# A dilated convolution with a gate: another order of the same instructions on five engines

## The chip, the cores and the metric

The kernel runs on one core of a Trainium2 chip. The metric is the device time of one execution in microseconds (us). A core has TensorE (PE in the profile, with its weight loads as PEld), VectorE (DVE), ScalarE (ACT), GpSimd (POOL) and SyncE (SP, which here only issues DMAs). Each engine works through its own instructions in the order in which they were written; engines wait for each other through semaphores.

## The reference

x is 2 x 16000 x 256, w is 3 x 256 x 512, w_o is 256 x 256, all bf16. A causal convolution of three taps, two time steps apart, is followed by a gate and a product:

```python
h = jnp.einsum('btc,cd->btd', xp[:, pad:pad + T, :], w[0])
for i in range(1, K):
    off = pad - i * dil
    h = h + jnp.einsum('btc,cd->btd', xp[:, off:off + T, :], w[i])
z = jnp.tanh(h[..., :D]) * _sigmoid(h[..., D:])
return z @ w_o
```

## The kernel before

Time is cut into 23 groups. A group of kind A has six phases of 256 time steps (18 groups), one of kind B four phases of 256 or 160 (4 groups); group 0 is done directly at the start. The convolution is computed by a short-convolution scheme that needs fewer products: sums and differences of the phases of x are multiplied by sums of the taps, and results are put together afterwards. A group has four blocks, one for each 128 of the 512 output channels.

A block of kind A goes through this, each letter being a token of the list below:

- F (PE) multiplies u1 by wa_sb into a PSUM bank "b"; c (ACT) copies it out as ss.
- M (PE) adds e (rm) times wm_sb into b; hh is then made from b, by h on DVE or by k on ACT.
- L (PE) adds f (rp) times wp_sb into b. A (DVE) makes a second bank "a" from ss and b. Y (DVE) makes yy from hh and b, or, after a k, from hh and a.
- Z (PE) adds u0 (r0) into b, once A and Y have read it; I (PE) adds u2 (ri) into a, once what reads a has read it.
- b, y and a (ACT) apply tanh or sigmoid to the three results.

A block of kind B has F, c, L, A, Z, I, b and a alone. Each of F, M, L, Z and I is two matmuls of up to 512 columns, here called a pair. After two such blocks g (DVE) multiplies th and sg into zz; P (PE) is four matmuls of 256 columns by w_o into a bank "o_ps"; e (ACT) or v (DVE) evicts it into osb; s (SP) stores, x (SP) loads by a transposing DMA. H and R are the last three P in two halves.

The operands of a group are tokens with a dot: `u2.7` is u2 of the A group with number 7. Written so, VectorE makes all of it. With `q` (`u2.7q22`) GpSimd makes one quarter, and not before the VectorE instruction that stands so many back has ended (`hold`). With `d` (`rm.15d`) GpSimd issues a DMA that adds one tile onto another: rm is e plus u3, rp is f plus u1, r0 is u0 plus uh, ri is u2 plus ud; u3, uh and ud are scaled copies of u1, made on VectorE. `wa.` are quarters of a weight sum. A GpSimd quarter after a DMA and a quarter waits for the one ahead of it (`settle`).

Three banks b, two banks a and three banks o_ps rotate; operands have three buffers (u3, uh, ud two), osb four.

What sets the order is one string, PLAN: 1730 tokens, read from left to right, each of which writes its instruction to its engine. Which block a letter stands for follows from ORDER, which gives the groups in turn. So the string sets the order on each engine, and also which of VectorE, GpSimd, GpSimd's DMA or ScalarE does a movable piece.

Of the kernel before, what the change touches and what calls it, by code (L numbers as in the profile page):

```python
# [22 lines left out]
wa.6q1 b L a G Z wa.14q10 F A b x wa.4q7 I c g P a d3.1 F L u1.0 c wa.0q1 Z A I b wa.13q1 P e.0 a Z f.0 F b P g I x
c uh.0 L e0 m.2 L d3.2q1 a F A e1 P d3.2q2 A c Z u0.0 I b I u3.0 a r0.0d Z u2.0 L p.2 b x d3.2q1 F e2 A P e3 F ud.0
c d0.2 Z a I u1.1 c L b g P d3.2q1 a L A e4 F wa.12q14 A Z wa.8q30 c e.1 I b Z g a L u1.2 b F wa.1q1 P e5 A ri.0d F
c rp.0 I e6 rm.0 L c s3 Z u3.1 a s2 M uh.1 s0 b uh.2 I x u2.1 k0 P a A F wa.7q1 e7 L u0.1 wa.9q11 P c A Z e8 wa.11q6
M ud.1 wa.15q28 b I Y k1 F f.1 a Z f.2 c I b L g x M a A F k2 u2.2 P u1.3q14 c L Y e9 M u1.3q54 A y I k3 rp.1d u3.2
P Y a Z L g e10 Z b A f.3q36 P y ud.2 F f.3q28 b Y P c r0.1d rm.1 P y Z ri.1d e.2 e11 F e.3 I b rm.2d M g c F k4 M
u0.2 u0.3q1 a L h5 c I y A f.3q12 L a M f.3q62 Y e12 P A u1.3q8 e13 Z I Y k6 u1.3q43 I b g ri.2d L a rp.2d F u3.3 y
Z A rm.3d c P u1.4 b r0.2d P a Y M rp.3d F y uh.3 Z ud.3 k7 v15 I b L u3.4 e14 ud.4 F f.4q68 c A P c M u0.3q20 Y a M  # L30
e.4 k8 Z k9 g L rm.4d b I u0.3q33 A e17 P a v16 F f.4q36 L y Y s8 P f.4q55 c x A Z y u2.4q74 M Y b I e18 h10 Z a F g
b P c L u2.3 F e19 u1.5 ri.3d M c A I u0.3q60 k11 M Y a L u0.4 y f.4q1 P A k12 I Z e20 r0.3d uh.4 Y P a rp.4d L b
f.5 r0.4d Z y A F b I g c P u2.5q72 y F Y M e21 u3.5 u2.5q4 I c v22 P y u2.4q90 h13 Z a u2.4q16 v23 M b L u2.4q50
h14 a s10 P s9 e24 u2.5q44 A F x y L Y e.5q82 P c A e.5q79 Z e25 Y M e.5q58 y I h15 b e.5q69 Z a g ri.4d F e26 L c I
A f.6q22 b P s11 uh.5 M a u2.5q82 Y F y rp.5d u0.5 P k16 Z e.6 e27 r0.5d L b g I c P u2.6q118 A y F M e28 u1.6q63 Y
P c f.6q1 h17 Z y I ud.5 e29 rm.5 M b s12 L h18 a u2.6q1 x F a P u2.6q45 A c L Y u1.6q20 e30 I A u1.6q108 e31 M Z a
Y u1.6q33 P k19 g ri.5d Z b L e32 u0.6 P f.7q89 y A I b F uh.6 u2.6q46 e33 P Y c F r0.6d u3.6 P y g rm.6d M e34 I
f.6q13 a h20 P c Z y u1.7 L f.6q67 b M A e35 P rp.6d Y F k21 s14 P a e.7 s13 Z c ud.6 I g e36 ri.6d L b M u2.7q71 A
e37 P a h22 F u0.7q137 e38 P Y u0.7q65 c L s15 Z y uh.7 x u2.7q72 A M b I f.7q90 h23 e39 F f.7q1 y Y L c f.7q114 I
v40 a Z u2.7q22 Y a M g P b P k24 A F e41 x L rp.7 e42 P c A Z y u1.8 I u0.8q93 b M Y a P u0.7q161 h25 Z y F uh.8 b  # L40
u3.7 I u2.8 s16 c rm.7d F e43 f.8 M c L g rp.8d k26 M a u2.7q76 A L k27 Y I y u0.8q1 A Z a u0.7q103 P v44 b u0.8q81
L Y y s17 P u0.8q162 A e45 F r0.7d e46 Z ud.7 Y c I ri.7d P b u3.8 r0.8d M u1.9 a Z e.8 k28 F b ud.8 L rm.8d e.9 c I
y g F u2.9q179 M y A P c P e47 h29 f.9q46 M a Y s18 f.9q43 L e48 s1 ri.8 u2.9q60 Z x k30 I A b L u2.9q117 Y a F y
u0.9q14 A Z c I g u0.9q1 b P a M Y F y u0.9q167 h31 I e49 ud.9 Z c u3.9 L b e.10 rm.9d M e50 A P u0.9q89 a F s19 h32
e51 I x Y f.9q75 c P g L a f.9q1 Z e52 Y P b M u0.10q72 A e53 F u1.10 Z c I h33 y P uh.9 b M f.10 s20 r0.9d y L h34
u2.9q136 F e54 A P a L c Y u0.10q111 I y Y u0.10q129 M e55 Z A rp.9d k35 P uh.10 ri.9d b Z g a I L e56 ud.10 u3.10 F
b s21 A P a x F u2.10 c P Y c M y u1.11 Z e57 M h36 b I u3.11 e58 L g u2.11q137 k37 F P a A L y Y u2.11q107 P c A
u2.11q42 Z y I f.11 rm.10d y M Y b u0.10q118 P e59 v60 rp.10d Z k38 s22 F uh.11 r0.10d b g P a L u0.11 c F P e61 A I
e62 ud.11 ri.10q1 M c Y P y r0.11d u1.12 Z y rp.11d M h39 b I e.11 e63 L u3.12 a F ri.10q1 h40 P e64 A P c ri.10q52
L e65 Y u2.11q33 M a s24 g ri.10q10 Z k41 x I b A L a F u2.12q103 Y y I u2.12q220 A c Z uh.12 rm.11d P y Y P b g M y  # L50
s23 F k42 v66 I u1.13q121 c Z v67 a ri.11d L f.12 e68 M b P A s25 e.13q152 P k43 x Y F a e.13q125 L c e.12 u1.13q170
Z e69 A I b M f.13 u1.13q1 e70 P Y a F u2.12q52 P v71 k44 Z c rp.12d g L y rm.12d M b A I k45 ud.12 P u2.13q69 Y a
s26 F e72 u0.12 L u2.13q15 c Z A P y u2.13q63 M Y b I u1.13q210 e73 h46 F a u2.12q15 Z c uh.13 rp.13d I g y L ri.12d
b M ud.13 P A k47 e.14q113 F a Y L c e.13q247 I A y Z e.14q191 e74 M Y e.13q189 P b h48 Z r0.12d y u3.13 F a g L
rm.13d b I f.14 c P u2.14q103 y F A e75 M v76 u0.13q202 I c h49 P u0.13q57 e77 M Y a u2.14q55 s28 L e78 h50 x
u0.13q102 Z a Y P u2.13q15 b L A e.14q70 y P y F u1.14 u0.13q101 Z A c I b ri.13d Y M e79 s27 F r0.13d u3.14 k51 g Z
c I u1.15 a L M b A f.15q131 P a u3.15 F f.15q226 e80 Y P k52 s29 e.15 P c x L g e81 Z y M A u0.15q78 b I h53
e.14q248 P y F Y e82 u2.15q170 L a u0.14 u2.15q128 Z c P Y b I u2.15q278 A e83 M rm.14d a ud.14 F h54 e84 Z rp.14d
uh.14 I c g L r0.14d b P e85 u2.14q287 A M y P Y e86 P h55 u2.14q38 y F u1.16 a Z ri.14d I g b L c P Y f.16q41 e87 F
e88 A M f.16q231 c P h56 u0.15q120 e89 Z v90 M a f.15q216 s32 L b s30 h57 u0.15q75 I x y A f.16q213 F a L Y f.15q45  # L60
y P uh.15 u0.15q94 c Z A e91 I s31 u2.15q110 Y M b P rm.15d g a F k58 rp.15d Z u3.16 c uh.16 L y u2.16 M b I ud.15 A
k59 P ri.15d F a ud.16 r0.15d Y L y P d0.3q55 c A Z e92 M Y b I u1.17 e93 d0.3q1 Z a h60 I m.3q93 b F e.16 ri.16d L
c g F rm.16d y P e.17q121 A c M e94 P h61 e95 M e.17q79 Y I a s34 f.16q22 L h62 s33 a Z A e96 d3.3q1 P y d0.3q64 Y P
e.17q45 b L g Z y rp.16d F b d3.3q40 Y I c P d3.3q65 A e97 F m.3q78 u0.16 e98 d0.3q252 M c I s35 h63 r0.16d Z a
u3.17 M e99 f.17 P b h64 L rp.17d a P A y u0.17q176 F e100 Y L y P d3.3q161 A u0.17q101 c Z Y I e.17q58 b I e101 g M
rm.17d a F s36 u2.17q5 h65 y P s4 s7 Z c g p.3q78 s5 L b M A e102 P u0.17q112 k66 Y F u2.17q17 a P v104 c L m.3q26
uh.17 p.3q67 Z e103 A M p.3q36 b s37 ud.17 I m.3q10 k67 Y P u0.17q286 a F v106 p.3q135 y L r0.17d Z c A P u2.17q16 y
M Y b I u2.17q30 e105 h68 Z a v107 F ri.17q5 b L ri.17q4 s38 y I A ri.17q3 P c Y F y ri.17q28 M c g Z a P h69 b P g
e108 M L e109 h70 F y I A c P a Y L I y Y Z a A M b P h71 y Z v110 F b L c I A F a L Y P c A I e113 v111 Z a L v112
Z b P A b s40 I g y s39 P a F I v114 c F P g c L a Z e115 A L P v116 b I e117 A Z s41 P g a s6 I b v118 Z a P b P  # L70
e119 g H P v120 s42 R P e121 H e123 v122 H R s44 R e124 s43 e125 s45
"""


# [572 lines left out]
```

## Time and profile before

| | |
|---|---|
| median of 3 runs | 258.78 us (258.61 to 259.19) |
| profiled execution | 258.77 us, span 256.6 us |
| granted TensorE clock | 0.995 |
| DVE busy | 242.8 us, 405 instructions |
| ACT busy | 243.7 us, 492 instructions |
| POOL busy | 176.9 us, 249 instructions |

The span runs from the first to the last instruction; the profiled execution has 2.2 us around it. A row of the timeline gives start and length in us, engine, line, operation, the written tile and the read ones, the shape, and the number of instructions that were merged; in brackets stands the engine's idle time ahead of it and what ended it. A row of the groups by line gives busy time and mean length in ns, then idle time ahead of the group and what ended it.

### The profile page before, as it was taken

How to read it: one execution, taken by the hardware profiler on the slowest of the kernel's cores; microseconds unless marked ns; L12 is line 12 of the kernel's file. 1: busy time of each engine (PE TensorE's matmuls, PEld its weight loads, DVE VectorE, ACT ScalarE, POOL GpSimd, SP SyncE). 2: the span in 40 equal slices, each digit the busy share in tenths (PEclk: the TensorE clock that was granted, in tenths of full speed). 3: DMA queues.
4: the chain of work that ended last, by engine and by line, in shares of the span. 5: the costliest groups of instructions: out<-in, count | busy, mean ns of one | idle time of the engine just before them, and what ended most of it. 6: DMA issues, size and time to landing. Idle time of an engine off the chain costs nothing.

```text
span 256.6 us, 4575 instructions
## 1 busy us (share of the span) xinstructions
PE 249.9 (97%) x1428; PEld 138.0 (54%) x1428; DVE 242.8 (95%) x405; ACT 243.7 (95%) x492; POOL 176.9 (69%) x249
## 2 busy tenths in 40 slices
...
GB/s 184 213 202 213 196 172 159 232 143 203 187 199 271 187 200 249 182 289 200 200 237 212 249 196 188 290 244 147 212 260 171 216 219 224 198 217 102 0 226 176
DMA packets 84320, 51.73 MB, mean 202 GB/s; under 512 B 69032, under 2 KB 70312, under 8 KB 84296
## 3 DMA queue, kind: packets, MB, share of 16 engines
...
q10 hardware_dynamic: 912, 0.95, 1.1%
q8 instruction: 11, 0.18, 0.3%
q14 instruction: 13, 0.11, 0.1%
...
## 4 chain that ended last, share of the span: by engine, by line
PE 82%; DVE 8%; DMA 3%; ACT 2%; issue 2%; ACTq 0%; DVEq 0%
PE b L359 48%; PE o_ps L478 18%; PE a L359 13%; DVE a L393 2%; DMA e<-u 2%; DVE zz L460 2%; DVE yy L393 2%; PE b L379 1%; PE a L379 1%; DMA xn<-in_x_dram 1%; DVE hh L393 1%; ACT osb L495 1%; ACT sg L441 1%; ACT th L441 0%; ACT ss L390 0%
## 5 line engine op out<-in xcount | busy, mean ns | idle before, releaser
L330 POOL TENSOR_TENSOR u<-xt 128x256 bf16<-128x256 bf16 x88 | 66.8, 774 | 15.0 <-PE b L359 8.4
L478 PE MATMUL o_ps<-wo_sb,zz 128*128 128x256 bf16 x496 | 72.0, 273 | 0.0
L495 ACT CAST osb<-o_ps 128x512 bf16<-128x512 f32 x101 | 63.8, 646 | 0.9 <-PE o_ps L478 0.7
L478 PEld LDWEIGHTS <-zz 128*128 128x128 bf16 x496 | 48.5, 98 | 27.6
L393 DVE SCALAR_TENSOR_TENSOR a<-ss,b 128x512 f32<-128x512 f32 (+1 forms) x88 | 59.5, 679 | 2.3 <-PE b L359 1.3
L390 ACT COPY ss<-b 128x512 f32<-128x512 f32 (+1 forms) x88 | 55.0, 628 | 0.9 <-PE b L359 0.6
L359 PEld LDWEIGHTS <-w_sb 128*128 128x128 bf16 x352 | 34.1, 97 | 35.1 <-issue 3.0
L359 PE MATMUL b<-e,wm_sb 128*128 128x512 bf16 x144 | 42.8, 379 | 0.3 <-DMA e<-u 0.3
L359 PE MATMUL b<-u,w_sb 128*128 128x512 bf16 x144 | 42.9, 379 | 0.2
L359 PE MATMUL b<-u,wa_sb 128*128 128x512 bf16 x144 | 42.9, 379 | 0.0
L359 PE MATMUL b<-f,wp_sb 128*128 128x512 bf16 x144 | 42.9, 379 | 0.0
L359 PE MATMUL a<-u,w_sb 128*128 128x512 bf16 x144 | 42.5, 379 | 0.3 <-DVE a L393 0.2
L460 DVE TENSOR_TENSOR zz<-th,sg 128x1536 bf16<-128x1536 bf16 (+2 forms) x46 | 41.3, 897 | 0.2
L441 ACT ACTIVATE th<-b 128x512 bf16<-128x512 f32 (+1 forms) x44 | 28.0, 636 | 1.4 <-ACT ss L390 0.7
L441 ACT ACTIVATE th<-a 128x512 bf16<-128x512 f32 (+1 forms) x44 | 28.6, 649 | 0.3 <-PE a L359 0.2
L441 ACT ACTIVATE sg<-b 128x512 bf16<-128x512 f32 (+1 forms) x44 | 28.0, 635 | 0.6 <-PE b L359 0.5
L441 ACT ACTIVATE sg<-a 128x512 bf16<-128x512 f32 (+1 forms) x44 | 28.3, 642 | 0.0
L359 PEld LDWEIGHTS <-wm_sb 128*128 128x128 bf16 x176 | 17.0, 98 | 17.2 <-DMA e<-u 1.2
L359 PEld LDWEIGHTS <-wp_sb 128*128 128x128 bf16 x176 | 16.9, 98 | 17.3 <-issue 1.6
L393 DVE SCALAR_TENSOR_TENSOR hh<-ss,b 128x512 f32<-128x512 f32 x38 | 25.9, 681 | 0.2
L393 DVE SCALAR_TENSOR_TENSOR yy<-hh,b 128x512 f32<-128x512 f32 x38 | 25.6, 678 | 0.0
L441 ACT ACTIVATE sg<-yy 128x512 bf16<-128x512 f32 x36 | 24.9, 693 | 0.7 <-DVE yy L393 0.7
...
## 6 DMA issues: line engine op xcount, KB each, us to landing
...
u<-uh POOLq DMA_DIRECT2D x18, 256.0 KB, 4.8
f<-u POOLq DMA_DIRECT2D x16, 256.0 KB, 4.7
u<-ud POOLq DMA_DIRECT2D x15, 256.0 KB, 4.6
e<-u POOLq DMA_DIRECT2D x15, 256.0 KB, 4.8
out_dram<-osb SPq DMA_DIRECT2D x8, 256.0 KB, 3.1
w_sb<-in_w_dram ACTq DMA_DIRECT2D x3, 256.0 KB, 4.1
xt<-in_x_dram SPq DMA_TRANSPOSE x22, 8.0
```

The lines of the kernel that those rows point to most:

```text
L330: ins = eng.tensor_tensor(out=o, in0=a, in1=b, op=op)
L359: nc.tensor.matmul(G[bank, oi][:, :2 * R], lhsT=wmat[:, ct, osl], rhs=G[mv][:, :, ct, :R], start=which == "first" and ct == 0, stop=ct == ...
L379: nc.tensor.matmul(G[bank, oi][:, :4 * r].rearrange("p (j r) -> p j r", j=4), lhsT=w_taps[tap][:, ct, osl], rhs=xt[:, j0:j0 + 4, ct, c0 + ...
L390: nc.scalar.copy(out=G["ss", oi][:, :n], in_=G["b", oi][:, :n])
L393: return note(nc.vector.scalar_tensor_tensor(out=out, in0=in0, scalar=scalar, in1=in1, op0=ALU.mult, op1=op))
L441: nc.scalar.activation(out=G[name, dt][:, j:j + 2, :R], in_=G[bank, oi][:, :2 * R].rearrange("p (q r) -> p q r", q=2), func=(ACT.Tanh, ACT ...
L460: note(nc.vector.tensor_tensor(out=G["z"][:, dt, :, :n], in0=G["th", dt][:, :, :n], in1=G["sg", dt][:, :, :n], op=ALU.mult))
L478: nc.tensor.matmul(o_ps[:, q, :], lhsT=z, rhs=wo_sb[:, dt, :], start=dt == 0 and (q == 0 or len(dts) == NT), stop=dt == NT - 1, skip_group ...
L495: copy(out=G["osb", at][:, 2 * jp:2 * jp + 2, :], in_=o_ps[:])
```

## The change

PLAN is replaced by another string of 1730 tokens. Groups, ORDER, buffers and functions stay. The diff's first line of the string:

```
-m.0 d3.0 p.0 F F d0.0 c F c G L w L A c D wa.5q2 D A wa.2q5 Z d0.1 I b D m.1 a L wa.3q1 F d A wa.10q2 Z c p.1 I
+m.0 p.0 d0.0 F F c G D c D d3.0 L w L A D wa.7q4 F A wa.2q6 d Z G I b p.1 Z c F m.1 a I d0.1 c L d3.1 b P wa.6q1 L a
```

By count of tokens, all of F, M, L, Z, I, P, H, R, c, A, Y, b, y, a, g, s and x are as many as before. These differ:

| token | before | after |
|---|---|---|
| h / k (hh on VectorE / ScalarE) | 38 / 34 | 36 / 36 |
| e / v (eviction on ScalarE / VectorE) | 103 / 23 | 102 / 24 |
| d3 whole / quarters | 2 / 8 | 3 / 4 |
| u0 whole / quarters | 10 / 32 | 11 / 28 |
| u2 whole / quarters | 7 / 44 | 5 / 52 |
| r0 by DMA / VectorE | 18 / 0 | 17 / 1 |
| rm by DMA / VectorE / quarters | 15 / 3 / 0 | 14 / 3 / 4 |
| ri by DMA / VectorE / quarters | 15 / 1 / 8 | 17 / 0 / 4 |

VectorE between hh and A of the second block of the A group with number 7, before (numbers are those of buffers):

```order
L393 SCALAR_TENSOR_TENSOR hh_1595<-ss_1569,b_1553 128x512
L328 TENSOR_SCALAR uh_1603<-u1_1576 128x1024
L328 TENSOR_SCALAR u3_1607<-u1_1406 128x1024
L330 TENSOR_TENSOR u2_1611<-xt_1284 128x1024
L330 TENSOR_TENSOR f_1621<-xt_1284 128x1024
L460 TENSOR_TENSOR zz_1536<-th6_1532,sg6_1582 128x1536
L393 SCALAR_TENSOR_TENSOR a_1637<-ss_1569,b_1553 128x512
L393 SCALAR_TENSOR_TENSOR yy_1643<-hh_1595,b_1553 128x512
```

And after:

```order
L393 SCALAR_TENSOR_TENSOR hh_1587<-ss_1564,b_1552 128x512
L328 TENSOR_SCALAR ud_1596<-u1_1379 128x1024
L487 CAST osb6_1602<-o_ps_1581 128x512
L393 SCALAR_TENSOR_TENSOR yy_1615<-hh_1587,b_1552 128x512
L393 SCALAR_TENSOR_TENSOR a_1623<-ss_1564,b_1552 128x512
L328 TENSOR_SCALAR uh_1632<-u1_1542 128x1024
```

Five instructions stood between hh and A; now three do, and Y is one of them.

GpSimd ahead of the DMA that makes rm of the A group with number 15 (`e<-u`), before:

```order
L330 TENSOR_TENSOR f<-xt 128x256 x2
L330 TENSOR_TENSOR u_2712<-xt 128x256
L330 TENSOR_TENSOR f<-xt 128x256
L330 TENSOR_TENSOR u_2712<-xt 128x256
L330 TENSOR_TENSOR f<-xt 128x256 x2
L330 TENSOR_TENSOR u_2712<-xt 128x256
L330 TENSOR_TENSOR u_2733<-xt 128x256
L325 DMA e<-u_2671 128x1024
```

And after:

```order
L330 TENSOR_TENSOR f<-xt 128x256
L330 TENSOR_TENSOR u_2749<-xt 128x256
L330 TENSOR_TENSOR u_2715<-xt 128x256 x2
L330 TENSOR_TENSOR u_2749<-xt 128x256
L330 TENSOR_TENSOR f<-xt 128x256 x3
L325 DMA e<-u_2828 128x1024
```

Nine quarters stood between it and the DMA before it; now eight do, and in the list the DMA stands 1.3 us of PE work further ahead of its M.

ScalarE at the very end, before:

```order
L495 CAST osb_3564<-o_ps 128x512
L495 CAST osb_3612<-o_ps 128x512
L493 CAST odd<-o_ps 128x256
L495 CAST osb_3636<-o_ps 128x512 x2
L642 UNCONDITIONAL_BRANCH
```

And after:

```order
L495 CAST osb_3609<-o_ps 128x512 x2
L493 CAST odd<-o_ps 128x256
L495 CAST osb_3636<-o_ps 128x512
L642 UNCONDITIONAL_BRANCH
```

The second half of the last tile (osb_3636) has left ScalarE; it is VectorE's last instruction after.

More of the change, by code (lines that the diff above doesn't have):

```diff
@@ L21 @@
 PLAN = """
-m.0 d3.0 p.0 F F d0.0 c F c G L w L A c D wa.5q2 D A wa.2q5 Z d0.1 I b D m.1 a L wa.3q1 F d A wa.10q2 Z c p.1 I
[L23 to L71, printed above, removed]
+m.0 p.0 d0.0 F F c G D c D d3.0 L w L A D wa.7q4 F A wa.2q6 d Z G I b p.1 Z c F m.1 a I d0.1 c L d3.1 b P wa.6q1 L a
@@ new lines @@
+A F wa.0q7 A x wa.4q6 I c g Z a L u1.0 b Z A e0 I b P u2.0 F a f.0 F c ud.0 Z c g L b I u0.0 wa.3q1 L A a F wa.8q22
+e1 A P wa.12q5 P c s0 m.2 Z e2 x e3 I d0.2 L b u3.0 Z a p.2 wa.1q1 F b A P c I g e4 Z d3.2 F b u1.1 I x a L e.0 c F
+A a P wa.9q1 c ud.1 L uh.0 I e5 u3.1 wa.5q1 Z A a L wa.14q37 b uh.1 P wa.10q3 A Z e6 ri.0d F g x b Z f.1 c I rm.0 b
+F L rp.0 c I u1.2 a M a P g k0 F A wa.13q1 e7 P e.1 L c wa.11q45 Z e8 A s2 I rp.1d b s3 r0.0 M a F Y wa.15q1 k1 P
+u2.1 c Z e9 g L ri.1d M b A y F uh.2 k2 P Y u1.3q19 c I u0.1 e10 L Z a u2.2 x u1.3q1 P y A M b u0.2 I k3 F Y a L
@@ new lines @@
+rm.1 c Z f.3q25 y I A M b r0.1d u3.2 P Y a F k4 e.2 Z c g L rm.2d b M e11 u1.3q40 A I e12 F h5 y P u1.3q1 Y L a P
+ud.2 c f.2 Z e13 M g b x u0.3q1 I k6 F A a L f.3q10 Y c I f.3q51 A e14 P y M uh.3 rp.2d Y Z a ri.2d P k7 u3.3 Z
+r0.2d u1.4 b L e.3 b F f.4q69 y A F c I v15 c f.3q31 P Y a M f.4q65 v17 M e16 rp.3d I k8 g Z rm.3d k9 L ud.3 a P
+u3.4 u2.4q1 b A L y F Y u0.3q12 y P A u0.3q36 c Z e18 I u0.3q80 Y M y e.4 r0.3d Z b P h10 a rm.4d F u2.3 b L c u1.5
+F x e19 M g c I e.5q62 k11 A M a L Y u2.4q35 y I A e.5q51 k12 P Z y Y f.4q9 L a uh.4 ri.3d I b f.5 Z s8 e20 u2.5q101
@@ new lines @@
+A F b P s9 u0.4 f.4q53 c P Y e21 F r0.4d g y M Z c rp.4d h13 P a u2.5q68 M v22 b L e23 F ud.4 y u2.4q16 h14 P c I
+u2.5q1 A e24 L u2.4q82 Y a M Y I u2.5q30 e25 Z k15 A e.5q80 P a uh.5 ri.4d Z b ud.5 L g y F f.6q13 e26 I A c P s11
+u3.5 u1.6q85 y P s10 Y M b ri.5d u0.5 Z a rp.5d F g k16 I b L e.6 u2.6q45 c P A e27 F e28 M u1.6q70 Y c P u1.6q117
+h17 y Z f.6q98 v29 M e30 L b f.6q8 h18 s12 I a x u1.6q61 Y F y L u2.6q35 A a P e.5q11 Y c Z e31 A P f.6q110 M b rm.5
+r0.5d I y g rp.6d F k19 Z a e.7 L c I u0.6 f.7q84 b P A e32 P uh.6 e33 M f.7q112 Y F a r0.6d u1.7 P e34 Z c h20 I
@@ new lines @@
+e35 g L b u2.7q72 s14 M a Y x F y P A u2.6q29 y P h21 Z c u3.6 P e36 g rm.6d L b I u0.7q28 e37 A F e38 P uh.7 c
+u2.6q26 Y s15 M e39 s13 M f.7q1 h22 a Z f.7q40 y I ud.6 L b u2.7q140 h23 P y u0.7q40 A F a L u2.7q50 Y e40 I c A
+u0.7q53 Z a M Y rp.7d b P u1.8 ri.6d k24 Z u3.7 y F g rm.7q77 L y I c A P e41 M rm.7q36 Y b s16 P u0.7q52 h25 a x Z
+y ud.7 F rm.7q1 v43 L b P u0.8q41 e42 Y F c u2.7q6 A I c M ri.7d uh.8 a e.8 Z r0.7d k26 M x g b I k27 L f.8 u0.8q1 F
+y A P a L u3.8 e44 Y P rm.7q1 c P A e45 f.9q10 Z e46 Y M u0.8q92 b I u2.8 rm.8d k28 Z u1.9 rp.8d F a I g b L y
@@ new lines @@
+u2.9q57 F A c P e47 f.9q72 M Y c P s18 u0.8q6 h29 e48 Z a uh.9 M ud.8 L b e.9 ri.8d I k30 A F f.9q78 y L Y a r0.8d I
+g c Z y M A b P h31 e49 P e50 F Y u0.9q1 L a s19 u1.10 Z c u2.9q39 s17 P A e51 M b u2.9q16 Y I y f.9q48 h32 F e52 P
+e.10 rp.9d c Z u3.9 a I g rm.9d M b L e53 u0.9q64 h33 F y s20 P u3.10 c u0.9q139 x Y P a M u0.9q69 A y L u2.9q145
+h34 e54 Z I Y y u2.10q25 L b uh.10 u2.10q8 P A a F u0.10q114 y Y Z c r0.9d A I b M g e55 Z k35 I e.11 a F ud.9 L b
+f.10 ri.9d P c A F u0.10q42 a M Y c P u0.10q115 e56 h36 Z y M u1.11 s21 b x L g k37 I F e57 A u2.11q167 P a u3.11
@@ new lines @@
+u0.10q68 L c Y I e59 u2.11q105 A M a Z u2.11q8 v58 k38 P Y u2.10q50 y P b L f.11 rp.10d Z y g rm.10d F e60 rm.11d I
+b A P u2.10q70 c v61 F a r0.10d M Y e62 P h39 y Z s23 u1.12 c I s6 L s22 b ud.10 x P ud.11 y ri.10q121 A F e63 M Y
+ri.10q45 c P a u0.11 ri.10q47 Z e64 M h40 b I uh.11 k41 L g u2.12q115 F a L A c P u2.12q172 Y y P e65 ri.10q57 A M y
+Z v66 u2.11q176 I k42 Y u2.12q83 P b L g rp.11d a Z y ri.11d F f.12 b P ud.12 u1.13q163 c I A e67 F Y a u1.13q222 M
+P c e.12 r0.11d Z k43 u0.12 M b rp.12 L e.13q1 k44 F A e68 I c v69 e.13q135 L s25 a P s24 Y u1.13q27 M e70 u3.12
@@ new lines @@
+u1.13q185 Z y A P k45 rm.12d g I b L e71 u2.13q159 Y F a P s26 f.13 e.13q157 c x Z A e72 I e.13q240 b M Y P a
+u2.13q66 h46 F y uh.12 Z c ud.13 L r0.12d uh.13 b M g rp.13d y I k47 e.14q27 F A P e73 Y L a u2.12q104 I v74 e75 Z c
+e.14q177 A s27 P y e.14q11 M Y b P u2.13q39 h48 a Z ri.12d f.14 e76 F b P u3.13 g L c rm.13d F y e.14q241 Y M c I
+h49 e77 M u0.13q123 y A P s28 u0.13q149 a x L h50 u0.13q237 y Z A L e78 u2.13q151 Y I b u2.14q121 P Y a F u0.13q81 y
+A Z c r0.13d I g b Z ri.13d M a u1.14 F b e.15 P rp.14d k51 F u3.14 c u1.15 L rm.14d e79 M A c u2.14q8 I e80 P Y k52
```

14 lines of the change are left out of this document (added).

## The prediction

> **What bounds the kernel now.** First the page, for the engines' shares and the chain.
>
> ```profile
> span 256.6 us, 4575 instructions
> PE 249.9 (97%) x1428; PEld 138.0 (54%) x1428; DVE 242.8 (95%) x405; ACT 243.7 (95%) x492; POOL 176.9 (69%) x249
> PE 82%; DVE 8%; DMA 3%; ACT 2%; issue 2%; ACTq 0%; DVEq 0%
> ```
>
> Three engines are nearly full, and the chain stays on PE for 82% of the span. A busy PE is not yet a full one, because matmuls overlap, so next I read starts in the timeline of PE (start, length, what), and counts in the groups by line.
>
> ```profile
> 5.22 2.63 PE L379 MATMUL b<-xt,w_sb 128*128 128x320 bf16 x18
> 7.68 0.45 PE L242 MATMUL tp<-ident,xn 80*128 80x80 bf16 x8
> 43.28 0.60 PE L478 MATMUL o_ps<-wo_sb,zz 128*128 128x256 bf16 x4
> 43.72 0.60 PE L359 MATMUL b<-u,w_sb 128*128 128x512 bf16 x2
> 44.15 0.60 PE L359 MATMUL b<-f,wp_sb 128*128 128x512 bf16 x2
> 250.20 1.47 PE L478 MATMUL o_ps<-wo_sb,zz 128*128 128x256 bf16 x12
> ...
> L478 PE MATMUL o_ps<-wo_sb,zz 128*128 128x256 bf16 x496 | 72.0, 273 | 0.0
> L478 PEld LDWEIGHTS <-zz 128*128 128x128 bf16 x496 | 48.5, 98 | 27.6
> L359 PE MATMUL b<-u,wa_sb 128*128 128x512 bf16 x144 | 42.9, 379 | 0.0
> L359 PE MATMUL b<-m,wm_sb 128*128 128x512 bf16 x24 | 6.8, 379 | 0.0
> L379 PE MATMUL a<-xt,w_sb 128*128 128x320 bf16 x24 | 3.8, 300 | 0.0
> ```
>
> From 43.72 to 44.15 a pair of 512 columns takes 0.432 us, from 43.28 to 43.72 four of 256 take 0.436, and from 5.22 to 7.68 eighteen of 320 take 0.137 each. Five groups of 144 and four of 24 make 408 pairs: 176.3 us. The 500 of 256 columns (496 and 4) make 54.5, the 80 of 320 columns 11.0, eight transposes 0.3. That is 242.1 us of work. It stands between 5.22 and 251.51 (250.20 and twelve times 0.109), which is 246.3. So PE stands still for some 4.2 us; this, and the 5.1 us from 251.51 to the end, is all that another order can shorten, since no matmul is added or taken away. The work before 5.22 has the same places in both lists.
>
> A rule weighed against this: the Trainium skill (Perfetto Trace Analysis, Identifying the Most-Contended Engine) says that matmul busy share is a bad measure and that the busy share of LDWEIGHTS and the share of peak FLOPs are good ones. By the first of these, 54% here, PE would have nearly half its time free; by its peak of 307.2 G elements a second, 571,392 columns by 128 in 256.6 us are an estimated 93%. The starts above side with the second, and the sum would otherwise have no floor.
>
> Where do the 4.2 us lie? A start later than the pitch allows is a gap. Those above 0.035 us, taken along the whole timeline:
>
> ```profile
> 42.31 0.59 PE L359 MATMUL b<-e,wm_sb 128*128 128x512 bf16 x2
> 42.85 0.59 PE L359 MATMUL a<-u,w_sb 128*128 128x512 bf16 x2
> 110.86 0.59 PE L359 MATMUL b<-f,wp_sb 128*128 128x512 bf16 x2
> 111.63 0.59 PE L359 MATMUL a<-u,w_sb 128*128 128x512 bf16 x2 [0.18 <-DVE a L393]
> 237.66 0.59 PE L359 MATMUL a<-u,w_sb 128*128 128x512 bf16 x2
> 238.25 0.59 PE L359 MATMUL b<-u,w_sb 128*128 128x512 bf16 x2
> ...
> 107.54 0.68 DVE L393 SCALAR_TENSOR_TENSOR hh<-ss,b 128x512 f32<-128x512 f32 x1
> 109.42 0.69 DVE L330 TENSOR_TENSOR f<-xt 128x1024 bf16<-128x1024 bf16 x1
> 110.02 0.95 DVE L460 TENSOR_TENSOR zz<-th,sg 128x1536 bf16<-128x1536 bf16 x1
> 110.89 0.69 DVE L393 SCALAR_TENSOR_TENSOR a<-ss,b 128x512 f32<-128x512 f32 x1
> ```
>
> First kind: Z and I, which wait for VectorE's A and Y. There are 13 such gaps, 2.03 us together, the first at 42.85 (0.11), the largest at 111.63 (0.34), the last at 238.25 (0.16). At 111.63 VectorE had finished hh at 108.2 and then did u-sums, f and zz before A.
>
> ```profile
> 12.59 1.07 PE L359 MATMUL b<-p,wp_sb 128*128 128x512 bf16 x4
> 13.50 0.71 PE L379 MATMUL a<-xt,w_sb 128*128 128x320 bf16 x4
> 202.79 0.59 PE L359 MATMUL b<-f,wp_sb 128*128 128x512 bf16 x2
> 203.28 0.59 PE L359 MATMUL b<-e,wm_sb 128*128 128x512 bf16 x2
> ```
>
> Second kind: F, M and L, which wait for ScalarE's copies and activations or for hh. 17 gaps, 1.41 us, from 13.50 (0.05) to 203.28 (0.06).
>
> ```profile
> 48.91 0.59 PE L359 MATMUL b<-e,wm_sb 128*128 128x512 bf16 x2
> 49.45 0.61 PE L359 MATMUL b<-f,wp_sb 128*128 128x512 bf16 x2
> 205.88 0.59 PE L359 MATMUL b<-u,w_sb 128*128 128x512 bf16 x2
> 206.81 0.61 PE L359 MATMUL b<-e,wm_sb 128*128 128x512 bf16 x2 [0.34 <-DMA e<-u]
> 201.43 0.87 POOL L325 DMA_DIRECT2D e<-u  x1
> e<-u POOLq DMA_DIRECT2D x15, 256.0 KB, 4.8
> ```
>
> Third kind: three waits for an accumulating DMA, 0.69 us: 0.11 at 49.45, 0.07 at 161.49, 0.50 at 206.81, where the issue at 201.43 was 5.4 us ahead.
>
> **The change part by part.** Only the list moves. By its tokens VectorE gets as many sums, two hh fewer and one eviction more: 0.6 us less at its steps (0.60 from f at 109.42 to zz, 0.87 from zz to A). ScalarE gets two hh more and one eviction fewer, 0.5 us more. I cost both at nothing, because each still has less to do than PE; should VectorE fall behind, its 0.6 us is already in the next term. GpSimd has 160 quarters of operands and 64 DMAs, as before.
>
> To compare the lists I count, for each edge, the PE work that stands between the producer's place and its consumer's. A tight edge has one pair or less, 0.432 us, while a VectorE operation takes 0.68.
>
> Z and I after A or Y: 20 tight edges before (14 for Z, 6 for I), 12 after (9 and 3). 2.03 us over 20 is 0.10 each; eight fewer give -0.81. Its ends are 0, if VectorE's total load and not the order makes the gaps, and -2.03. I take the count, because at 111.63 the delay was visibly work put ahead of A, and after has there only one ud, an eviction and Y.
>
> F, M and L after ScalarE or hh: 75 tight before (22, 30, 23), 91 after (37, 34, 20). 1.41 over 75 is 0.019 each; sixteen more give +0.30. Ends: 0 and +1.3, if every new one costs what the mean gap does (0.083).
>
> DMAs: the three late ones get longer leads (6.06, 6.06, 4.33 us become 9.52, 14.29, 5.63), which takes 0.69 away. New short leads stand at r0.1 and r0.16 (both 4.33 us). Before had three at 4.33 and one of them cost 0.50, so 0.17 each: +0.34. Net -0.35; ends -0.69 and +0.31 (two times 0.50).
>
> Last quarters: rm.7 and ri.10 now end on GpSimd 0.87 us of PE work ahead of M and I; before, the nearest such were 1.30 and 1.73, and cost nothing.
>
> ```profile
> L330 POOL TENSOR_TENSOR f<-xt 128x256 bf16<-128x256 bf16 x28 | 20.8, 754 | 3.5 <-PE b L359 2.8
> 127.82 2.02 POOL L330 TENSOR_TENSOR f<-xt 128x256 bf16<-128x256 bf16 x2
> 198.80 1.30 POOL L330 TENSOR_TENSOR f<-xt 128x256 bf16<-128x256 bf16 x2
> 128.22 1.08 DVE L460 TENSOR_TENSOR zz<-th,sg 128x1536 bf16<-128x1536 bf16 x1
> ```
>
> A quarter takes 0.75 and fits into 0.87 if GpSimd starts it at its place. I take +0.15, a little over the nearer end, 0; the other is the first rival's. rm.7's last quarter also waits for u3 on VectorE, and f.9's quarter stands behind it with long leads.
>
> The end:
>
> ```profile
> 249.88 0.69 DVE L487 CAST osb<-o_ps 128x512 bf16<-128x512 f32 x1
> 251.49 1.07 ACT L495 CAST osb<-o_ps 128x512 bf16<-128x512 f32 x2 [0.34 <-PE o_ps L478]
> ```
>
> Two evictions run one behind the other on ScalarE until 252.56, then the last store. After puts the last on VectorE. PE's last matmul ends at 251.67 (twelve steps and the drain, 250.20 and 1.47), so it would run from about 251.71 for 0.69, until 252.40: -0.15. Ends: -0.5, a whole one of ScalarE's two, and +0.2, what VectorE's 0.69 is above that. Stores and loads on SP keep their number and sizes and I cost their moves at nothing, covered by four output buffers; if one were late, an eviction and then P would wait.
>
> Sum: -0.81 + 0.30 - 0.35 + 0.15 - 0.15 = -0.86. Against this execution's 258.77 (span 256.6 and 2.2 around it; the median is 258.78) that is 257.9.
>
> **The rivals.** Slower: GpSimd runs late at rm.7 and ri.10 (near 106 and 146 us). Beside zz two quarters took 2.02, against 1.30 beside instructions that read PSUM. If one further quarter is ahead of each, PE waits 0.75 to 1.4 twice, 1.5 to 2.8 in all. It decides from 1.5, because without the 0.15 the rest is -1.0: 259.3 to 260.6, middle 259.9. For it: the leads of 0.87. Against: GpSimd is 69% busy. The Trainium skill (GPSIMD Engine Reference, Specifications) says that GpSimd shares its SBUF interfaces with VectorE instructions that have two SBUF inputs, which is what zz is; 2.02 against 1.30 agrees.
>
> Gaps only move: after has VectorE do 0.9 us more while PE works from its 40th to its 60th microsecond (20.8 for 19.9 by the list and those steps). If all of it becomes gaps, +0.9 cancels the sum: 258.8. For it: the gaps at 42.85 and 49.45 lie in that stretch already. Against: later stretches get less.
>
> More than counted: Z and I lose three quarters of their 2.03 and all DMA waits go: -1.5 + 0.3 - 0.69 - 0.15, 256.7. For it: the leads from L to I grow from 6.4 to 7.1 pairs in the mean. Against: VectorE is as full as ever.
>
> PSUM turns late: F's 37 tight edges cost 0.08 each for the fifteen new, +1.2 in place of +0.3: 258.8. For it: some F now stands directly behind the activation that frees its bank. Against: the 22 of before cost 0.38 together.
>
> **How the numbers follow.** Forecast 0.46 (its own range 257.2 to 258.6), more than counted 0.14, gaps only move 0.14, late GpSimd 0.20, PSUM 0.06. The measurement tells 0.2%, 0.5 us. Of the forecast 0.38 lies below 258.25 and 0.08 within; gaps only move and PSUM are within but for 0.03; late GpSimd is slower. Faster 0.38 + 0.14 = 0.52, same 0.08 + 0.17 = 0.25, slower 0.20 + 0.03 = 0.23. Leaving a tenth on each side, the range goes from 256.5, just past the better case, to 260.1, into the upper half of the late GpSimd.
>
> **What would show it.** Right: gaps ahead of Z and I sum to 1.2 us, no DMA wait at rm.15, the last osb eviction on VectorE ends 0.75 us after PE's last matmul. Wrong: waits of M or I for a GpSimd sum near 106 or 146 us, or gaps of a u-product between 45 and 65 us.

## The result, and the profile after

The changed list is slower: 260.98 us (260.82 to 262.10, four runs) against 258.85 for the kernel before beside it, a ratio of 1.0088 (95% interval 1.0067 to 1.0109). A second series gave 260.41 (ratio 1.0075, 1.0059 to 1.0091). Ratios here and below are worked out over the executions, without those more than 1.5% above the fastest of their kernel, and so can differ from the quotient of the medians. I had forecast 257.9 and a range up to 260.1. The profiled execution took 261.01 us, with a span of 259.1 (before: 258.77 and 256.6): the span grew by 2.5, the time by 2.24. From the page of the kernel after:

```profile
span 259.1 us, 4578 instructions
PE 251.0 (97%) x1428; PEld 138.5 (53%) x1428; DVE 243.3 (94%) x404; ACT 243.8 (94%) x493; POOL 174.3 (67%) x249
PE 73%; DVE 13%; ACT 5%; DMA 4%; issue 3%; DVEq 0%; ACTq 0%
```

The busy times are those of before to within 1.1 us on every engine but GpSimd, and there they are less. What moved is the chain: PE carries 73% of it in place of 82%, VectorE 13% in place of 8%. PE's starts, read as in the prediction, give gaps of 6.0 us after the first token of the list, 4.3 before. Counted along PE's work since the list's first matmul, the gaps between 120 and 160 us (some 134 to 176 on the timeline) grew from 0.61 to 2.23 us, and all other stretches together changed by 0.1. So nearly all of the net loss lies in one stretch. Elsewhere gains and losses cancel: between 80 and 100 us the gaps fell from 0.93 to 0.42, between 180 and 200, where rm.15 is waited for, they grew from 0.62 to 0.92. The large gaps of the kernel after, in PE's timeline:

```profile
134.01 0.59 PE L359 MATMUL b<-u,wa_sb 128*128 128x512 bf16 x2
134.89 0.59 PE L359 MATMUL b<-u,w_sb 128*128 128x512 bf16 x2 [0.29 <-DVE a L393]
...
143.11 0.59 PE L359 MATMUL b<-e,wm_sb 128*128 128x512 bf16 x2
144.06 0.59 PE L359 MATMUL b<-u,w_sb 128*128 128x512 bf16 x2 [0.35 <-DVE yy L393]
...
208.00 0.59 PE L359 MATMUL a<-u,w_sb 128*128 128x512 bf16 x2
209.34 0.60 PE L359 MATMUL b<-e,wm_sb 128*128 128x512 bf16 x2 [0.75 <-ACT sg L441]
```

A pair takes 0.43, so the Z at 134.89 is 0.45 late and the Z at 144.06 0.52. The M at 209.34 is 0.91 late; the row names ScalarE, but it is rm.15's accumulating DMA, which landed at 209.29. Now VectorE and GpSimd ahead of the two Z:

```profile
129.74 0.69 DVE L393 SCALAR_TENSOR_TENSOR hh<-ss,b 128x512 f32<-128x512 f32 x1
130.35 0.66 DVE L328 TENSOR_SCALAR u<-u 128x1024 bf16<-128x1024 bf16 x1
133.32 0.92 DVE L328 TENSOR_SCALAR uh<-u 128x1024 bf16<-128x1024 bf16 x1
140.29 0.87 DVE L330 TENSOR_TENSOR u<-xt 128x1024 bf16<-128x1024 bf16 x1
142.54 0.87 DVE L328 TENSOR_SCALAR u<-u 128x1024 bf16<-128x1024 bf16 x1
145.73 0.90 DVE L330 TENSOR_TENSOR f<-xt 128x1024 bf16<-128x1024 bf16 x1
...
129.76 4.95 POOL L330 TENSOR_TENSOR u<-xt 128x256 bf16<-128x256 bf16 x7
141.62 3.58 POOL L330 TENSOR_TENSOR u<-xt 128x256 bf16<-128x256 bf16 x5 [1.01 <-PE a L359]
```

And the same operations in the kernel before:

```profile
135.56 0.42 DVE L328 TENSOR_SCALAR uh<-u 128x1024 bf16<-128x1024 bf16 x1
137.13 0.41 DVE L328 TENSOR_SCALAR u<-u 128x1024 bf16<-128x1024 bf16 x1
139.26 0.68 DVE L330 TENSOR_TENSOR u<-xt 128x1024 bf16<-128x1024 bf16 x1
140.46 0.41 DVE L328 TENSOR_SCALAR u<-u 128x1024 bf16<-128x1024 bf16 x1
143.56 0.69 DVE L330 TENSOR_TENSOR f<-xt 128x1024 bf16<-128x1024 bf16 x1
...
134.00 1.20 POOL L330 TENSOR_TENSOR u<-xt 128x256 bf16<-128x256 bf16 x2
140.78 2.86 POOL L330 TENSOR_TENSOR u<-xt 128x256 bf16<-128x256 bf16 x3 [3.83 <-PE a L359]
```

A scaled copy of 0.41 takes 0.66 to 0.92 after, a sum of 0.69 takes 0.87 to 0.90. In the kernel after GpSimd makes seven quarters from 129.76 to 134.7 and five from 141.6 to 145.2, and all but the last of these instructions run beside one; f.11 at 145.73 runs beside DMA issues alone. Further on, at 159.18, the copy ud.12 takes 1.29 beside two quarters. Over the whole span VectorE's instructions on SBUF are stretched by 4.6 us after and 4.0 before, nearly the same. Only the place differs: between 120 and 160 us of the timeline, where VectorE works almost without a break in both kernels, it is 2.5 us after and 0.3 before.

### The profile page after: what moved, and what is told of

Same layout as the page of the kernel before. It is cut to its first block, busy times and chain, and to the rows that moved or that the text cites. A ratio compares the mean times of both kernels' runs of the same rounds, so it can differ in the third digit from the quotient of the medians.

```text
span 259.1 us, 4578 instructions
## 1 busy us (share of the span) xinstructions
PE 251.0 (97%) x1428; PEld 138.5 (53%) x1428; DVE 243.3 (94%) x404; ACT 243.8 (94%) x493; POOL 174.3 (67%) x249
## 4 chain that ended last, share of the span: by engine, by line
PE 73%; DVE 13%; ACT 5%; DMA 4%; issue 3%; DVEq 0%; ACTq 0%
PE b L359 43%; PE o_ps L478 15%; PE a L359 11%; DVE a L393 3%; DMA e<-u 2%; DVE yy L393 2%; DVE hh L393 2%; ACT th L441 2%; PE b L379 1%; PE a L379 1%; ACT osb L495 1%; DVE u L330 1%; DMA xn<-in_x_dram 1%; DVE zz L460 1%; ACT sg L441 1%
## 5 line engine op out<-in xcount | busy, mean ns | idle before, releaser
L330 POOL TENSOR_TENSOR u<-xt 128x256 bf16<-128x256 bf16 x92 | 68.1, 757 | 8.9 <-PE a L359 2.7
L460 DVE TENSOR_TENSOR zz<-th,sg 128x1536 bf16<-128x1536 bf16 (+2 forms) x46 | 40.5, 882 | 0.0
L441 ACT ACTIVATE sg<-b 128x512 bf16<-128x512 f32 (+1 forms) x44 | 28.7, 652 | 1.6 <-PE b L359 1.4
L441 ACT ACTIVATE th<-b 128x512 bf16<-128x512 f32 (+1 forms) x44 | 28.7, 653 | 0.5 <-PE b L359 0.5
L441 ACT ACTIVATE sg<-a 128x512 bf16<-128x512 f32 (+1 forms) x44 | 28.9, 657 | 0.2 <-PE a L359 0.2
L393 DVE SCALAR_TENSOR_TENSOR yy<-hh,a 128x512 f32<-128x512 f32 x36 | 24.5, 681 | 1.0
L441 ACT ACTIVATE th<-yy 128x512 bf16<-128x512 f32 x36 | 25.4, 705 | 0.0
L393 DVE SCALAR_TENSOR_TENSOR hh<-ss,b 128x512 f32<-128x512 f32 x36 | 24.4, 678 | 0.9 <-PE b L359 0.6
```

What stands on the lines that cost most here:

```text
L330: ins = eng.tensor_tensor(out=o, in0=a, in1=b, op=op)
L393: return note(nc.vector.scalar_tensor_tensor(out=out, in0=in0, scalar=scalar, in1=in1, op0=ALU.mult, op1=op))
L441: nc.scalar.activation(out=G[name, dt][:, j:j + 2, :R], in_=G[bank, oi][:, :2 * R].rearrange("p (q r) -> p q r", q=2), func=(ACT.Tanh, ACT ...
L460: note(nc.vector.tensor_tensor(out=G["z"][:, dt, :, :n], in0=G["th", dt][:, :, :n], in1=G["sg", dt][:, :, :n], op=ALU.mult))
```

## The experiments

Theory 1: GpSimd's quarters stretch VectorE's instructions beside them, and where VectorE has no slack PE waits. Theory 2: the order itself loads VectorE there. Theory 3 is rm.15's late DMA: it is issued late (3), it queues behind a store (3b), or it waits for the transposing load ahead of it (3c). Theory 4 is what the start and the end of the execution add. Each run has executions of the kernel before beside it, and the ratios are to these.

**after_again.** No edit.

> The changed list itself, once more, as the base for the runs beside it. Theory 1 (VectorE's SBUF instructions are stretched by GpSimd quarters beside them at 120 to 160 us, where the order leaves VectorE no slack): the same stretched copies and the same gaps of PE there, 1.5 us at 120-140 and 0.7 at 140-160 within 0.3, and 260.9 +- 0.4 us. If the overlaps come from chance, the gaps wander by more than 0.5 us between profiles. The start (0.45 us more until the first token of the list) is the same code as before's up to there: should it be gone here, it was that execution's, not the list's.

260.41 us. Gaps of 1.53 at 120 to 140 and 0.71 at 140 to 160 came back, with the same copies (0.67, 0.92, 0.87, 0.87), so this is no accident of one execution. The 18 matmuls at the start took from 4.93 to 7.39, which is 2.46 us, not the 2.89 of the first profile: the start was that execution's.

**held.** Five GpSimd quarters are let go later, each behind the VectorE instruction that it ran beside; a smaller number behind q, or a later place, does this.

```
-u0.9q64 h33 F y s20 P u3.10 c u0.9q139       +h33 F y s20 P u3.10 u0.9q0 c u0.9q0
-uh.10 u2.10q8                                +uh.10 u2.10q0
-u0.10q115 e56 h36 Z y M u1.11                +e56 h36 Z y M u1.11 u0.10q0
-u3.11 u0.10q68     -ud.12 u1.13q163          +u3.11 u0.10q0     +ud.12 u1.13q0
```

> The changed list with five GpSimd quarters between 120 and 165 us held back until VectorE's scalar copy beside them is done (u3.10, uh.10, u1.11, u3.11, ud.12). The same instructions in the same order on VectorE, ScalarE and PE. Theory 1 (contention between GpSimd and VectorE makes the gaps there): those copies return to 0.42 us, PE's gaps at 120-160 fall from 2.2 us to about 1.0, time 259.7 (259.3 to 260.2). Theory 2 (the order itself, VectorE's steps ahead of A, Y and hh, makes them): the gaps stay within 0.3 us, time 260.6 to 261.1.

259.57, a ratio of 1.0037 (1.0023 to 1.0050) beside 1.0075: 0.84 us back, nearly half of the loss, though the sum forecast 1.2. Timeline of held:

```profile
129.73 0.42 DVE L328 TENSOR_SCALAR u<-u 128x1024 bf16<-128x1024 bf16 x1
132.56 0.50 DVE L328 TENSOR_SCALAR uh<-u 128x1024 bf16<-128x1024 bf16 x1
145.12 1.42 DVE L460 TENSOR_TENSOR zz<-th,sg 128x1536 bf16<-128x1536 bf16 x1
...
130.24 3.35 POOL L330 TENSOR_TENSOR u<-xt 128x256 bf16<-128x256 bf16 x5 [0.79 <-DVE u L328]
145.16 2.05 POOL L325 DMA_DIRECT2D e<-u  x2
146.26 1.65 POOL L330 TENSOR_TENSOR u<-xt 128x256 bf16<-128x256 bf16 x1
...
134.63 0.59 PE L359 MATMUL b<-e,wm_sb 128*128 128x512 bf16 x2
135.06 0.59 PE L359 MATMUL b<-u,w_sb 128*128 128x512 bf16 x2
```

Four of the five instructions get their usual length or nearly so (u3.10 0.42, uh.10 0.50, u1.11 0.69, ud.12 0.41); the copy u3.11 still takes 0.88 beside another quarter. The Z that was 0.45 late (here at 135.06) is on time. Between 120 and 140 the gaps fall from 1.53 to 1.28 only, because later waits grew in its place: an I at 148.38 is 0.48 late behind the zz at 145.12, which took 1.42 instead of 0.95. Between 140 and 160 they fall from 0.71 to 0.31, after that from 0.32 to 0.10. So held keeps 1.6 us of gaps between 120 and 160, where the kernel before has 0.6, and no run isolates what makes this rest.

**rm15_early.** `rm.15d` goes from behind `s5` to right behind `u2.15q194`, ahead of three quarters.

> The changed list with the accumulating DMA rm.15 issued ahead of three quarters of f.15 and f.16 instead of behind them (about 4.5 us earlier). Theory 3 (the late issue is the wait of 0.91 us at 209.3): the wait is gone, time -0.9 to -0.5, 260.1 to 260.5; the rest is unchanged. Rival: those three quarters end later now and f.15 or f.16 become what PE waits for, or VectorE and not the DMA was the limit there: -0.2 to +0.3.

261.05 (1.0098, 1.0071 to 1.0125), no faster than after_again: the rival. No wait for rm.15 in its profile, but the three quarters now start as VectorE turns to u1.16, zz and u1.17. Its timeline, and below it the same two operations in after_again:

```profile
204.82 1.42 DVE L460 TENSOR_TENSOR zz<-th,sg 128x1536 bf16<-128x1536 bf16 x1
207.09 1.30 DVE L330 TENSOR_TENSOR u<-xt 128x1024 bf16<-128x1024 bf16 x1
...
213.91 0.60 PE L359 MATMUL b<-f,wp_sb 128*128 128x512 bf16 x2 [0.46 <-DVE hh L393]
```

```profile
202.57 0.95 DVE L460 TENSOR_TENSOR zz<-th,sg 128x1536 bf16<-128x1536 bf16 x1
...
204.37 0.69 DVE L330 TENSOR_TENSOR u<-xt 128x1024 bf16<-128x1024 bf16 x1
```

That is 1.08 us on VectorE, and 1.37 us of new gaps of PE from 209 to 215. This profile (262.82 us, the slowest of six) also carries waits of 1.1 and 1.0 us for the DMAs of rm.6 and ri.12, which the move doesn't touch.

**held_early.** Both edits.

> The five held quarters and the early rm.15 together. If theories 1 and 3 both hold, the gains add: 1.2 + 0.7 = 1.9 us, time 259.0 (258.6 to 259.6), which is the time of the kernel before. Theory 2 with theory 3: 260.2 to 260.6. If neither: 260.9.

259.97 (1.0058, 1.0038 to 1.0079): the gain of held, less what rm15_early loses.

**before_collide.** The converse, in the list of before: six quarters let go later, so that the second of each pair is under way as VectorE turns to SBUF.

```
-u0.10q111 … u0.10q129 … uh.10                +u0.10q1 u0.10q0 uh.10
-u3.11 … u2.11q137 … u2.11q107                +u2.11q1 u2.11q0 u3.11
-u2.11q42 Z y I f.11 … u0.10q118              +Z y I u2.11q1 u0.10q0 f.11
```

> The list of before, with six GpSimd quarters between 125 and 146 us let go later, so that the second of each pair starts as VectorE turns to a copy or a sum in SBUF (uh.10, u3.11, f.11). VectorE, ScalarE and PE have the order of before. Theory 1 (contention, where VectorE has no slack, is what costs): the three instructions become 0.3 to 0.5 us longer each, new gaps of PE at 125-150 of 0.6 to 1.2 us, time 259.1 to 259.8 against 258.5. Theory 2 (the changed order alone makes its gaps; before's has room there): stretched instructions but 258.3 to 258.8.

260.15 (1.0061, 1.0049 to 1.0073): 1.4 us slower, more than forecast. Timeline:

```profile
135.74 1.38 DVE L460 TENSOR_TENSOR zz<-th,sg 128x1536 bf16<-128x1536 bf16 x1
141.04 1.42 DVE L460 TENSOR_TENSOR zz<-th,sg 128x1536 bf16<-128x1536 bf16 x1
...
143.70 0.59 PE L359 MATMUL b<-u,w_sb 128*128 128x512 bf16 x2 [0.49 <-DVE yy L393]
...
163.21 0.60 PE L359 MATMUL b<-e,wm_sb 128*128 128x512 bf16 x2 [0.92 <-ACT osb L495]
```

It was zz and not the copies that got longer, by 0.9 in all, with 1.0 us more gaps between 120 and 140. A second 1.08 is the M at 163.21, which waited for rm.11's DMA; that was issued 0.7 us later by the clock and landed after 7.1 us instead of 6.1. So letting quarters run beside VectorE, with PE's, VectorE's and ScalarE's order as it was, makes before slower in this place by about 1 us; the rest is a DMA.

**unload.** v58 and v61 become e58 and e61.

> The changed list, with two evictions at 141 to 147 us (v58, v61) on ScalarE instead of VectorE; the contention stays. Theory 2 (VectorE's load by the list is the limit there): VectorE is 1.2 us lighter, the gaps at 140-160 (0.7 us) go, those at 134.9 and 144 (1.0 us) stay or halve: time -0.6 to -1.0, 259.5 to 259.9. Theory 1 alone (the stretched copies, not the load): -0.3 to 0. Rival: ScalarE, 94% busy, falls behind and PE waits for its copies: +0.3 or more.

260.06 (1.0060, 1.0047 to 1.0073), a gain over after_again's 1.0075 that the intervals don't separate. Timeline of PE:

```profile
133.89 0.59 PE L359 MATMUL b<-u,w_sb 128*128 128x512 bf16 x2 [0.29 <-DVE a L393]
143.06 0.59 PE L359 MATMUL b<-u,w_sb 128*128 128x512 bf16 x2 [0.35 <-DVE yy L393]
150.02 0.59 PE L359 MATMUL b<-u,wa_sb 128*128 128x512 bf16 x2 [0.21 <-ACT th L441]
```

The two large waits stay (0.45 and 0.51), the later ones for VectorE (0.08, 0.17, 0.30) go, and an F now waits 0.37 for ScalarE. So the load has a part in what follows 148 us, none in the two large waits.

**stores.** `s5` behind `ri.15d`; at the end `R H e123 e122 s44 H R s43 R e124 v125 s45` for `H H e122 R H R e123 s43 R e124 s44 v125 s45`, with the first H ahead of the last P.

> The changed list with only the place of stores moved: s5 (256 KB, old data) goes behind ri.15's DMA instead of just ahead of rm.15's, and the odd store at the end goes out ahead of s43, right after its eviction. Theory 3b (rm.15 is late because it queues behind 256 KB that could wait, 1.2 us): rm.15 lands about 5.4 us after its issue instead of 6.6, and PE's wait of 0.91 us goes. Theory 4 (the last 0.34 us at the end come from the odd store's late issue): from PE's last matmul to the end 4.9 instead of 5.2. Both: -1.2, 259.2 (258.9 to 259.7). If the DMA's lateness comes from its own work and the end from the last store: 260.3 to 260.6.

260.32 (1.0075, 1.0048 to 1.0102), and held with the same edit (**held_stores**) 259.87 (1.0043, 1.0029 to 1.0057):

> The five held quarters and the moved stores together. If theories 1, 3b and 4 explain the loss, their gains add: 0.84 + 0.9 + 0.3, so 258.4 (258.0 to 258.8), the time of the kernel before. If VectorE's load (theory 2) is a cause of its own, 0.5 or more stays: 259.0 or above.

Neither part answers as forecast. SP has nothing to wait for between rm.15's place and ri.15's, so s5 went out at 201.9 all the same, ahead of the DMA, which landed after 6.9 us; 3b was not tried by this. And the odd store issued 0.4 us ahead of PE's end changed nothing there: 5.2 us from there to the end of the span, as in the other profiles of the changed list (5.2 to 5.3). What does stand ahead of rm.15 is on SP in the kernel after, and the answer on DMAs for 202.6 to 203.2 shows the traffic:

```profile
200.06 1.85 SPq L167 DMA_TRANSPOSE xt<-in_x_dram  x1
```

```profile
DMA packets 566, 0.14 MB, mean 241 GB/s; under 512 B 566, under 2 KB 566, under 8 KB 566
...
e<-u POOLq DMA_DIRECT2D x1, 256.0 KB, 6.6
```

As rm.15 is issued, all packets under way are below 512 B: the last load of x, which transposes and was begun 2.6 us ahead of it.

**x_late.** `x` from ahead of `b P Y u2.15q194` to behind `s5`.

> The changed list with the last transposing load of x moved from ahead of the stores s32 and s5 to just behind them, so that rm.15's accumulating DMA is no longer some 2.6 us behind it. Theory 3c (accumulating DMAs that follow a transposing load wait until it is through; the bandwidth is near nothing for about 1.5 us around it): rm.15 lands 4.5 to 5.2 us after its issue instead of 6.6, PE's wait of 0.8 to 1.2 us goes: 259.4 to 259.8. If the sheer bytes in the queue are what it waits for: at most -0.3, 260.1 to 260.5; rp.15 and ri.15, now behind the load, may be late instead.

259.51 (1.0034, 1.0015 to 1.0054). SP, then PE, then the DMA:

```profile
203.00 4.01 SPq L167 DMA_TRANSPOSE xt<-in_x_dram  x1
...
207.12 0.59 PE L359 MATMUL a<-u,w_sb 128*128 128x512 bf16 x2
207.55 0.59 PE L359 MATMUL b<-e,wm_sb 128*128 128x512 bf16 x2
```

```profile
e<-u POOLq DMA_DIRECT2D x1, 256.0 KB, 4.2
```

M comes 0.43 behind the pair ahead of it: no wait. Against after_again's 1.0075, in another series, some 1.0 us come back, which is the wait. The packets in the traces show the order in which the data moved. The load consists of 1408 packets of 256 bytes. In the kernel after they start between 202.4 and 205.4 us, and the first packet of rm.15's DMA starts at 206.9, 4.2 us after its issue, behind those of two stores as well. In x_late the small packets start from 205.9 on, and rm.15's first one 1.5 us after its issue. The times spread more (258.75 to 262.66), and the profiled execution, 261.76, has a wait of 2.14 us for r0.16's DMA at 226.5, which no other profile has.

**before_x.** The same load in before, from behind `u0.15q75 I` to behind `s31`.

> The list of before with only the last transposing load moved behind the store s31, about 3 us later, beside rm.15's issue instead of 2.7 us ahead of it. Theory 3c: rm.15 lands within 4.8 us instead of 5.3, the wait of 0.5 us at 206.8 goes: 258.1 (257.9 to 258.4). Otherwise 258.4 to 258.8, or slower by a new wait for ri.15 or the quarters of the last group.

258.60 (1.0001, 0.9989 to 1.0013). It doesn't test the theory: SP reached the load at 200.94, still ahead of rm.15's issue at 201.32, which landed after 5.2 us; the wait was 0.39. The load's packets (from 202.7 to 204.9) were again ahead of rm.15's first one, at 204.7.

**held_unload**, **held_unload_x.** To held are added `f.11 u2.10q0` for `u2.10q50 … f.11`, `u2.10q1` for `u2.10q70`, and e58; the second has the late load too.

> The five held quarters, two more of u2.10 at 144 to 147 us let go so that they don't run into f.11 and zz, and the eviction v58 on ScalarE. Theory 1 with theory 2 (contention and load together make the gaps of 120-160): those gaps fall from 1.6 (held) to 0.5 to 0.8 us, as in the kernel before, time 258.5 to 259.0, with only rm.15's wait left above it. If the load by the list doesn't matter: as held, 259.4 to 259.8.

> The same with the late x load. If theories 1, 2 and 3c hold together: 257.7 to 258.3, below the kernel before. Without 3c: 258.5 to 259.0.

261.62 (1.0115, 1.0099 to 1.0131) and 261.07 (1.0113, 1.0078 to 1.0148): both slower, a miss. Timeline of held_unload:

```profile
144.58 1.35 POOL L330 TENSOR_TENSOR u<-xt 128x256 bf16<-128x256 bf16 x1 [0.65 <-DVE f L330]
145.89 0.87 POOL L325 DMA_DIRECT2D f<-u  x1
146.47 2.06 POOL L325 DMA_DIRECT2D e<-u  x2
...
151.82 0.59 PE L359 MATMUL b<-e,wm_sb 128*128 128x512 bf16 x2 [1.71 <-DMA e<-u]
```

The held quarter stands in GpSimd's queue ahead of three DMAs; rm.10's was issued 1.3 us later than in held and took 1.0 us longer to land (5.3 for 4.3), so M waited 1.87, and Z for r0.10 another 1.09. All waits of Z and I for A or Y, though, came to 0.53 us in the whole list. rm.15's wait is 0.97 us in the first of the two runs and none in the second.

**held_x**, **held_x_e58**, **held_x_e58_u3.** Held with the late load; then e58; then u3.11's quarter `u2.11q167` behind it as well.

> The changed list with the five held quarters and the late x load. If the two causes add, 260.4 - 0.84 - 0.9 = 258.7 (258.3 to 259.1), the time of the kernel before within what can be told; gaps of PE 4.0 to 4.5 us, as before's 4.3. If they share a wait (what one gives back, the other takes): 259.3 to 259.7.

> The same with the eviction v58 on ScalarE, 0.6 us less for VectorE at 143. If VectorE's load is a third cause: I and L at 148 to 149 (0.65 us of gaps in held) come on time, -0.4 to -0.6 against the run beside it, 258.1 to 258.4, below the kernel before. If not: within 0.2 of it, or up to +0.4 if ScalarE's copies fall behind.

> The same, and u3.11, still 0.88 us long beside the quarters of u2.11 in held, is left alone: they go behind it. Contention: u3.11 takes 0.42, another -0.2 to -0.4 at 142 to 144 (Z waits for Y there, 0.27 us in held). Rival: the quarters, and with them rm.10's DMA behind them, get 0.4 us later, and M waits for that DMA at 150: +0.2 to +1.

260.16 (258.76 to 261.93; 1.0051, 1.0026 to 1.0076), 258.91 (257.87 to 261.60; 1.0012, 0.9986 to 1.0039) and 261.37 (1.0081, 1.0056 to 1.0107). The third is the rival again: rm.10's DMA late by 1.88. In held_x rm.15's wait is gone, but there is a new one, here in ScalarE's waits and in PE's timeline:

```profile
ACT osb L495 <- DMA out_dram<-osb: 1.1, 1, 1.1
```

```profile
134.66 0.59 PE L359 MATMUL b<-u,wa_sb 128*128 128x512 bf16 x2 [0.98 <-ACT th L441]
```

An eviction waited for its buffer: the store issued at 124.98 landed after 6.7 us, in held after 2.3, although the two lists are the same up to 200 us. The store at this place was late in the profiles of held_early (6.4 us) and held_x_e58 (7.2 us, and an F 1.63 late) too. Without this 1.15 and the 0.19 behind it the execution's 260.05 would be 258.7, the forecast; three of its twelve runs are at 258.8 to 259.0. That the others carry the same wait is likely and not shown; by the medians the two edits together give no more than either alone. held_x_e58 is level with the kernel before within what can be told, and nothing here beats it; whether e58 itself has a part in that stays open, since its interval and that of held_x overlap and the profiles of both have the late store.

## Why the prediction was wrong, by its steps

- **Z and I after A or Y, -0.81: wrong in sign.** 14 gaps, 2.60 us, in place of 13 and 2.03: +0.57. This is the step that failed. The count was right as far as it goes: on tight edges there were 11 gaps with 1.77 us before, and 7 with 1.29 after. But seven others, 1.31 us, stand on edges with 0.86 us of PE work or more between, where before had two (0.26). I counted places in a list and took a VectorE instruction for its usual length. With a copy of 0.87 instead of 0.41 ahead of its Y, the Z at 144.06 was 0.52 late on a lead of two pairs. The term had no price for what GpSimd does beside VectorE. I gave the count a lower end of -2.03 and an upper one of 0; nothing in the sum could go above.
- **F, M and L, +0.30: right in sign, too small.** 2.11 in place of 1.41, +0.69. ScalarE's share is +0.09, though its tight edges grew by sixteen; +0.61 is hh on VectorE, again the stretched queue, and held takes 0.5 of it back.
- **DMAs, -0.35: wrong, +0.44.** 1.13 us in place of 0.69. rm.15's longer lead (5.63 for 4.33) didn't help, because its landing took 6.6 us instead of 5.3. I read the wait of before as a short lead; x_late shows that in the changed list it is the load ahead. In the kernel before the trace says the same: the load's row begins 2.7 us ahead of rm.15 and lasts until 201.86, its packets start between 201.9 and 204.2, and the first packet of rm.15's DMA starts at 204.0, 2.6 us after its issue. No run moves that load far enough to show it by a time. The new short leads of r0.1 and r0.16 cost nothing in this profile, and in two later ones 0.08 and 2.14.
- **Last quarters, +0.15: 0.** rm.7 and ri.10 came 0.43 and 0.15 us ahead of need. So the rival of a late GpSimd, 259.9, fell at its place; but its row, zz beside quarters, and the page named there pointed at the mechanism. I followed it from VectorE to GpSimd, not the other way.
- **The end, -0.15: +0.33.** The eviction did move: it ended 0.73 after PE's last matmul, as forecast. Yet from there to the end of the span it took longer; of this 0.06 lies ahead of the last store's landing and 0.28 behind it. before_collide, with before's end, also shows 1.57 us behind the landing in place of 1.28, and before_x 1.28. What sets it stays open.
- **The start, 0: +0.41** in this profile; the later ones of both lists lie between 0.4 less and 0.5 more than before's 11.30 for the first token's matmul, so it is the execution's, as the prediction had it.

PE's last matmul began 2.17 us later: 0.41 at the start and 1.76 in gaps, of which the first three terms are 1.70. With the end's 0.33 that is the 2.5 by which the span grew; the time around the span was 0.27 less in this execution. The rival that gaps only move had its stretch named wrongly: at 40 to 60 us they went from 0.28 to 0.55, and the loss lies at 120 to 160.

What is shown: holding five quarters gives 0.84 us back, putting quarters beside VectorE in the old list costs about 1 us in the same stretch, and moving the last load gives some 1.0. Of that 1.0 only 0.41 is loss against the kernel before (0.91 for 0.50), which has the wait as well; the 1.0 us of gaps that held keeps above before between 120 and 160 has no cause shown. The Trainium skill (Advanced Engine Details and Errata, VectorE Performance Modes) says that VectorE's second SBUF port is shared with GpSimd and that GpSimd instructions and VectorE's two-port ones block each other; 0.92 us for a copy of 0.41 agrees. That both gains add up is worked out for one execution with a late store, and fits the three fastest; it is not shown for the others.
